# Cosine attention followed by a gated MLP: 73 narrow dummy matmuls become nine, seven of them 512 columns wide

## The chip, the cores and the metric

The kernel runs on one core of one Trainium2 chip. The metric is the device time of one launch in microseconds, as the median of several runs; lower is better. Three runs of the kernel before gave 273.07, 273.60 and 273.94 us, median 273.6.

## What is computed

Linear attention with cosine weights over 8 batches of 8 heads (576 positions, head size 64), then a two-layer MLP (512 to 2048 to 512) with a gate `h * sigmoid(beta * h)`:

```python
r = np.maximum(x, 0.0)                                   # phi(x), for q and k
phi = np.concatenate([r * cos_w, r * sin_w], axis=-1)
kv  = np.einsum('bhsf,bhsd->bhfd', k_p, v)
z   = np.sum(k_p, axis=2)
num = np.einsum('bhsf,bhfd->bhsd', q_p, kv)
den = np.einsum('bhsf,bhf->bhs', q_p, z)[..., None] + 1e-06
x   = (num / den).transpose(0, 2, 1, 3).reshape(4608, 512)
h   = x @ w_in
out = (h / (1 + np.exp(-beta * h))) @ w_out
```

## The kernel before

The 4608 tokens of the MLP are worked on in nine chunks of 512, each about one batch of attention long. TensorE (PE) does all products: k against v (`kv_mm`, L276), q against that result (`num_mm`, L297), both layers of the MLP (L386 and L621, and from the third chunk on a scheme with fewer products, L511 and L563) and many transposes. VectorE (DVE) and ScalarE (ACT) clip, scale, divide and move results out of PSUM; GpSimd (POOL) helps. All operations are issued in an order written by hand; each engine works through its own instructions in that order, and waits on semaphores where it needs another engine's result or a DMA.

The change concerns the first microseconds. While the first loads (`raw_q`, `raw_v`, `raw_k`, issued from the queue of SP in that order: q, first half of v, first half of k, second half of v, the rest of k, then weights) are on their way, this happens:

- DVE writes zeros into a tile of 512 columns that is later the tile S1 (the profile calls it S): 128 columns first (L145), two small constants (L147, L149), then the other 384 (L160). ACT makes cos and sin, DVE makes tan of the positions (L176).
- PE runs dummy matmuls on these zeros, by `warm_pe(count, w, bank)` at L673: `count` matmuls of a 128x128 weight of zeros on `w` columns of zeros (default 512), each overwriting `w` columns of one PSUM bank that nobody reads. L685 issues 58 of 48 columns, L700 six of 128, L701 nine of 48, and L704 one of 512.
- Between them stand real operations. L689: nine fp32 transposes that spread tan over the partitions; DVE copies the result to `tanr` (L694). L692: a transpose of beta. L235: nine transposes of the first half of q, after DVE clipped it to `qb` (L193), and nine of the second half after L704. ACT copies the turned q (L240), DVE multiplies it by `tanr` (L223).
- `warm_long` (L679) runs two more dummies, in fp32 on real columns of q; each shows as two matmuls in the trace.
- Then the first real products: L276 (kv of the first two heads of each group, waiting for k clipped by ACT, L192, and DVE, L193), ACT's copy (L286), L297, DVE's division (L308, L312, L319), the transposes of its result (L356), and the MLP's first layer (L386).

```python
zeros = S1.rearrange("q i t -> q (i t)")[:, 0:512]
nc.vector.memset(zeros[:, 0:P], 0.0)
...
nc.vector.memset(zeros[:, P:512], 0.0)
```

## Time and profile before

| | |
|---|---|
| median of 3 runs | 273.6 us (273.07 to 273.94) |
| span of the profiled execution (first to last instruction) | 272.7 us |
| PE busy, matmuls | 265.3 us, 97% |
| PEld busy (weight loads, overlapping PE) | 206.8 us, 76% |
| DVE busy | 224.0 us, 82% |
| ACT busy | 188.4 us, 69% |
| POOL busy | 68.3 us, 25% |

The span is of one profiled execution; its whole device time is not listed apart from the three runs. A line of the page or of the timeline names the line of the kernel (L675 is line 675), the engine, the operation, what is written from what, the sizes, and how often (x58). In the timeline the first two numbers are the start and the length in microseconds of a run of like instructions; the bracket at the end gives how long the engine was idle before it and who released it. A matmul's end is modelled: its record contains the drain of the array, so records of consecutive matmuls overlap, and the distance between two starts says what one costs. The chain of waits follows the execution back from its last instruction, at each step to what released it.

### The profile page before, as it was taken

To read this page: it belongs to the slowest core of one execution; us is meant where nothing else is said; L and a number is where in the kernel's file an instruction comes from. 1 tells how busy PE (TensorE), PEld (TensorE's weight loads), DVE (VectorE), ACT (ScalarE), POOL (GpSimd) and SP (SyncE) were. 2 spreads that over 40 slices of the span, in tenths; PEclk is the share of its full clock that TensorE was granted. 3 is DMA by queue.
4 is the path that set the end of the run, shared out by engine and by line. 5 is a ranking of instruction groups with operands and counts; after the bars stand their busy time and mean duration, and the time that the engine had idled before them with its cause. 6 is when DMAs were issued, how large, how long until landed. Compare 5 with 4: busy or idle time off the path is not lost.

```text
span 272.7 us, 8970 instructions
## 1 busy us (share of the span) xinstructions
PE 265.3 (97%) x3712; PEld 206.8 (76%) x3712; DVE 224.0 (82%) x596; ACT 188.4 (69%) x384; POOL 68.3 (25%) x89
## 2 busy tenths in 40 slices
PE   8899999999899999999999999999999999999994
PEld 8554455455784588888888888888888888888883
DVE  5989969499989889789989997899589768757852
ACT  4778777796419656899489966996696179428920
POOL 1444000510078000660085009300840060000001
PEclk9999999999999999999999999999999999999999
DMA  6999999999969999994589439943600570015005
GB/s 237 374 395 383 392 390 319 379 201 336 284 130 311 240 348 226 240 313 103 147 216 370 92 58 223 332 71 62 181 2 2 61 185 1 2 27 130 0 2 155
DMA packets 50681, 54.00 MB, mean 198 GB/s; under 512 B 31232, under 2 KB 31760, under 8 KB 50640
## 3 DMA queue, kind: packets, MB, share of 16 engines
q1 hardware_dynamic: 47504, 45.55, 59.1%
q0 software_dynamic: 2784, 7.61, 9.6%
q8 instruction: 29, 0.48, 0.7%
q10 hardware_dynamic: 352, 0.27, 0.4%
q14 instruction: 12, 0.10, 0.1%
HBM read 36.71 MB, written 9.44 MB: 169 GB/s over the span
## 4 chain that ended last, share of the span: by engine, by line
PE 85%; DVE 9%; DMA 3%; SPq 1%; issue 1%; ACT 1%; DVEq 0%
PE ps L621 32%; PE ps L511 27%; PE ps L386 10%; PE ps L544 5%; PE ps L563 4%; PE ps L297 3%; DMA raw_v<-in_v_dram 3%; PE ps L276 3%; DVE vb L219 1%; DVE xs L319 1%; DVE qs L223 1%; SPq L79 1%; DVE S L406 1%; DVE rk L193 1%; DVE qb L193 0%
## 5 line engine op out<-in xcount | busy, mean ns | idle before, releaser
L537 POOL DMA_DIRECT2D out_dram<-o_sb x58 | 33.9, 591 | 147.3 <-ACT o_sb L658 86.3
L420 ACT ACTIVATE g_t<-ps,beta 128x512 bf16<-128x512 f32 x96 | 60.3, 702 | 1.4 <-PE ps L511 1.3
L621 PEld LDWEIGHTS <-S 128*128 128x128 bf16 x448 | 43.4, 98 | 5.2
L511 PE MATMUL ps<-w_stage 128*128 128x256 bf16 x288 | 46.6, 272 | 0.1
L386 PE MATMUL ps<-xt,win 128*128 128x512 bf16 (+1 forms) x196 | 42.8, 375 | 0.1
L511 PEld LDWEIGHTS <-w_stage 128*128 128x128 bf16 x384 | 37.3, 98 | 5.1 <-issue 0.2
L487 DVE TENSOR_TENSOR ps<-ps,p 128x256 f32<-128x256 f32 x74 | 30.5, 428 | 8.6 <-PE ps L511 3.0
L394 ACT ACTIVATE g_t<-ps,beta 128x512 bf16<-128x512 f32 x48 | 32.3, 688 | 7.2 <-PE ps L386 7.1
L621 PEld LDWEIGHTS <-g_t 128*128 128x128 bf16 x336 | 32.3, 98 | 4.5 <-ACT g_t L420 0.4
L386 PEld LDWEIGHTS <-win 128*128 128x128 bf16 x196 | 18.7, 98 | 21.1 <-issue 0.5
L511 PE MATMUL ps<-xt,win 128*128 128x256 bf16 x192 | 32.9, 273 | 0.0
L511 PEld LDWEIGHTS <-win 128*128 128x128 bf16 x288 | 28.0, 98 | 3.4
L621 PE MATMUL ps<-wout,g_t 128*128 128x256 bf16 x224 | 28.9, 273 | 0.0
L406 DVE TENSOR_TENSOR S<-g_t 128x512 bf16<-128x512 bf16 (+1 forms) x66 | 25.7, 418 | 3.3 <-ACT g_t L420 1.7
L480 ACT COPY ps<-ps 128x256 f32<-128x256 f32 x62 | 22.6, 383 | 7.5 <-PE ps L621 4.0
L217 ACT ACTIVATE vb<-raw_v,sin 128x256 bf16<-128x256 f32 (+1 forms) x58 | 26.0, 503 | 1.5 <-DMA raw_v<-in_v_dram 1.5
L621 PE MATMUL ps<-T,S 128*128 128x256 bf16 x224 | 26.6, 273 | 0.0
L621 PE MATMUL ps<-wout,S 128*128 128x256 bf16 x224 | 26.4, 273 | 0.0
L319 DVE TENSOR_TENSOR xs<-ps,rden 128x768 bf16<-128x768 f32 (+4 forms) x26 | 22.8, 884 | 0.9 <-DVE rden L312 0.2
L223 POOL TENSOR_TENSOR qs<-qt,tanr 128x1152 bf16<-128x1152 bf16 x6 | 14.3, 2387 | 27.4 <-PE ps L563 21.0
L658 ACT COPY o_sb<-ps 128x512 f32<-128x512 f32 x11 | 6.3, 587 | 20.1 <-PE ps L621 20.1
L487 DVE TENSOR_TENSOR ps<-ps,u 128x256 f32<-128x256 f32 x36 | 15.3, 427 | 5.3 <-PE ps L511 3.3
(112 smaller groups left out, 414.7 us busy)
## 6 DMA issues: line engine op xcount, KB each, us to landing
raw_v<-in_v_dram SPq DMA_DIRECT2D x7, 1152.0 KB, 9.7
raw_k<-in_k_dram SPq DMA_DIRECT2D x7, 1152.0 KB, 9.5
raw_q<-in_q_dram SPq DMA_DIRECT2D x7, 1152.0 KB, 7.4
out_dram<-o_sb POOLq DMA_DIRECT2D x58, 128.0 KB, 4.5
w_stage<-in_moe_w_in_dram SPq DMA_DIRECT2D x3, 1024.0 KB, 12.8
w_stage<-in_moe_w_out_dram SPq DMA_DIRECT2D x2, 1024.0 KB, 7.9
w_stage<-in_moe_w_out_dram SPq DMA_DIRECT2D x4, 512.0 KB, 11.9
out_dram<-o_sb SPq DMA_DIRECT2D x10, 128.0 KB, 2.4
```

Source lines behind the costliest of these rows:

```text
L217: got = nc.scalar.activation(o, a, AF.Copy, scale=t[:, n : n + 1])
L223: return eng.tensor_tensor(dst.rearrange("q n (g p) -> q n g p", g=2), src.rearrange("q n (g p) -> q n g p", g=2), tanr[:, n0:n1].unsqueez ...
L319: nc.vector.tensor_tensor(o.rearrange("q j n s d -> q j (n s) d"), nv[:, :, a:z, :, 0:D].rearrange("q j n s d -> q j (n s) d"), rden[:, :, ...
L386: nc.tensor.matmul(ps[:, h_bank(c, jt), i * 64 : (i + w) * 64], lhsT=win[jt // 4][:, mi, (jt % 4) * P : (jt % 4 + 1) * P], rhs=xt[:, i : i ...
L394: return nc.scalar.activation(gs[c, jt // 4][:, jt % 4], ps[:, h_bank(c, jt)], AF.Silu, scale=beta[:, jt : jt + 1])
L406: return nc.vector.tensor_tensor(o, l, r, op=op)
L420: return nc.scalar.activation(gs[c, jt // 4][:, jt % 4], bank, AF.Silu, scale=beta[:, jt : jt + 1])
L480: return nc.scalar.copy(at("a", 0), at("b", 0))
L487: nc.vector.tensor_tensor(dst, at("b", 0), st["p5"], op=ALU.add)
L511: nc.tensor.matmul(dst, lhsT=l[:, g], rhs=r[:, :, g * HP : (g + 1) * HP], start=start and g == 0, stop=g == 1, skip_group_check=True)
L537: (eng or own).dma_start(out=out_v[bb, n][:, m0:m1], in_=o_sb[hf * HP : (hf + 1) * HP, m0:m1])
L621: nc.tensor.matmul(dst, lhsT=l(i), rhs=r[:, i], start=start and i == 0, stop=i == order[-1], skip_group_check=True)
```

## The change

Two places in the first microseconds. The 58 dummies of 48 columns ahead of the tan transposes become five of 512 columns. The six of 128 and nine of 48 columns ahead of the first q transposes become two of 512 and two of 48. Banks and positions in PE's order stay; the dummy at L704 and `warm_long` stay.

```diff
-    warm_pe(58, 48)
+    warm_pe(5)
...
     q_relu(0, 1)
-    warm_pe(6, 128, bank=2)
-    warm_pe(9, 48, bank=2)
+    warm_pe(2, bank=2)
+    warm_pe(2, 48, bank=2)
     q_turn_pe(0, 0, 4)
```

In columns, the first group goes from 58 x 48 = 2784 to 5 x 512 = 2560, the second from 6 x 128 + 9 x 48 = 1200 to 2 x 512 + 2 x 48 = 1120. PE has 64 matmuls and 64 weight loads less. The first wide dummy reads all 512 zero columns, and so waits for the memset at L160; the first narrow one read 48 and waited for an earlier one.

## The prediction

> **What bounds the kernel now.** I read the page first, then the windows, then the chain of waits, then the timeline of each engine up to 20 us.

> ```profile
> span 272.7 us, 8970 instructions
> PE 265.3 (97%) x3712; PEld 206.8 (76%) x3712; DVE 224.0 (82%) x596; ACT 188.4 (69%) x384; POOL 68.3 (25%) x89
> PEclk9999999999999999999999999999999999999999
> q8 instruction: 29, 0.48, 0.7%
> ```

> ```profile
> 19.00:69.00 50.00, 49.99 (x687) 26.21 (x684) 42.59 (x92) 39.00 (x66) 7.65 (x12) 1.00 1.05 346
> 71.00:269.00 198.00, 197.91 (x2690) 167.88 (x2688) 164.19 (x461) 135.67 (x290) 52.94 (x60) 1.00 0.59 147
> ```

> The windows (the columns are length, then PE, PEld, DVE, ACT and POOL busy, granted clock, DMA share, GB/s) show PE busy for 49.99 of 50 us and for 197.91 of 198. So from 19 us on the kernel is a solid block of TensorE work; the change touches nothing in it. What the change can move is the moment at which that block begins. The chain says what sets that moment:

> ```profile
> 3.16 9.06 DMA raw_v<-in_v_dram
> 12.22 0.02 issue
> 12.25 0.92 DVE vb L209
> ...
> 17.54 1.06 DVE xs L319 x2
> ...
> 18.65 0.40 PE ps L356 x4
> 19.04 3.03 PE ps L386 x18
> ```

> Up to 12.22 us it is a load, the second half of v (raw_v); from there to 18.6 us a run of VectorE work; PE takes over only at 18.65. The dummies, all before 7 us, are not in the chain.

> **The change on the timeline.** The PE rows of that stretch (start, length, what):

> ```profile
> 0.99 2.50 PE L675 MATMUL ps<-S 128*128 128x48 bf16 x58 [0.99 <-DVE zero_b L149]
> 3.56 1.19 PE L689 MATMUL ps<-identf,tan 64*128 64x64 f32 x9
> 4.68 0.29 PE L692 MATMUL ps<-identf,beta 16*128 16x16 f32 x1
> 4.90 1.18 PE L675 MATMUL ps<-S 128*128 128x128 bf16 x15
> 5.94 1.14 PE L235 MATMUL ps<-ident,qb 128*128 128x128 bf16 x9
> 6.88 0.63 PE L675 MATMUL ps<-S 128*128 128x512 bf16 x1
> 7.30 1.17 PE L235 MATMUL ps<-ident,qb 128*128 128x128 bf16 x9
> 8.26 2.30 PE L679 MATMUL ps<-raw_q,S 128*128 128x512 f32 x4
> 11.25 0.70 PE L276 MATMUL ps<-vb,rk 64*64 64x130 bf16 x36 [0.69 <-ACT rk L192]
> ...
> 16.81 1.46 PE L386 MATMUL ps<-xt,win 128*128 128x512 bf16 x6
> ...
> 22.26 7.94 PE L386 MATMUL ps<-xt,win 128*128 128x512 bf16 x36
> ```

> ```profile
> L675 PE MATMUL ps<-S x74: 214/215/634, 1.0 to 6.9; 128*128 128x48 bf16 x67, 128*128 128x128 bf16 x6, 128*128 128x512 bf16 x1
> L679 PE MATMUL ps<-raw_q,S x6: 592/592/1017, 8.3 to 13.6; 128*128 128x512 f32 x6
> ```

> *Prices.* A record's length contains its drain, so I price by the distance between starts. Narrow: (2.50 - 0.215) / 57 = 0.040 us. Wide: the one wide bf16 dummy starts at 6.88 and the next transpose at 7.30, so 0.42 us. The same 512 columns cost 7.94 / 36 = 0.22 us at 22 us. So before about 8.3 us PE runs at half its later rate, though the granted clock row shows full speed everywhere; the row evidently has nothing for this stretch, and I trust the spacing. The fp32 dummies of L679 date the turn: the longest, 1017 ns, is the first, and 592 the usual, so the rate doubled while they ran, between 8.3 and about 9.1 us.

> *First group, line 685.* Removed: 58 x 0.040 = 2.32 us. Added: 5 x 0.42 = 2.10 us. One wait is added. A narrow dummy reads 48 zero columns, which the first memset writes; a wide one reads all 512, so the first now waits for the second memset. DVE:

> ```profile
> 0.89 0.06 DVE L149 MEMSET zero_b<- 128x1 f32 x1
> 0.94 0.22 DVE L160 MEMSET S<- 128x192 uint32 x1
> ...
> 3.25 0.17 DVE L176 TENSOR_TENSOR tan<-eps,sin 128x9 f32<-128x9 f32 x1
> ...
> 4.36 0.85 DVE L694 COPY tanr<-ps 128x320 f32<-128x320 f32 x2 [0.37 <-PE ps L689]
> 5.13 0.75 DVE L193 TENSOR_SCALAR qb<-raw_q 128x1152 bf16<-128x1152 f32 x1
> ...
> 12.25 1.35 DVE L209 TENSOR_TENSOR vb<-raw_v,ps 128x1152 bf16<-128x1152 f32 x1 [0.19 <-DMA raw_v<-in_v_dram]
> ```

> That memset ends at 0.94 + 0.22 = 1.16; PE started 0.04 us after the one it waited for (0.89 + 0.06 to 0.99), so now about 1.20 in place of 0.99. Behind the waiting dummy stand only dummies and the L689 transposes. The wide group is through at 1.20 + 2.10 = 3.30. The transposes read tan, ready at 3.25 + 0.17 = 3.42, and began at 3.56; they keep 3.56 with 0.2 us to spare. On the path: 0. If a wide one cost its whole record (0.63) at the end, it would end at 1.20 + 4 x 0.42 + 0.63 = 3.51, still before 3.56. At the full rate (0.22) it ends at 2.3, and PE just idles. What would a miss cost? The tanr copy at 4.36 waits for these transposes, and DVE then has 0.19 us of idle before its 12.25 entry, where it waits for the load anyway; a delay d costs d - 0.19.

> *Second group, lines 700 and 701.* Removed: 6 of 128 and 9 of 48 columns, from 4.90 to 5.94, 1.04 us. Added: 2 x 0.42 + 2 x 0.040 = 0.92, so done at 5.82. The q transposes behind it read qb, which DVE has at 5.13 + 0.75 = 5.88, and started 0.06 after that. They stay at 5.94. Path: 0; the earliest they could gain is under 0.06, and the load at 12.22 hides it.

> *What is issued.* 64 matmuls and their 64 weight loads fall away, 128 PE instructions. The orders of POOL and SP are unchanged and those of DVE and ACT keep each instruction in its place. No DMA is moved past another.

> *The turn of the rate.* No row shows what makes it turn, so I bound it. Total dummy time before 6 us falls from 2.32 + 1.04 to 2.10 + 0.92 us, a tenth, in the same places; PE streams in both from 4.9 us to the L679 dummies with no pause above 0.1 us. I take an unchanged turn: 0. Earlier: the transposes of L235 would end earlier, but DVE, ACT and POOL all wait at 12.2 us for raw_v, so 0 as well. Later: the first rival.

> [...]

> *Sum.* 0 (first group) + 0 (second) + 0 (instructions) + 0 (rate) on the span of 272.7 us. The profiled execution's span lies 0.9 us below the median of the runs, 273.6, which I take as what lies around it plus run-to-run spread (0.87 us from 273.07 to 273.94). Forecast: 273.6 us, no change that can be told.

> **Rivals.**

> *A. The rate turns later; slower.* For it: the dummies begin 0.21 us later, are a tenth shorter, and the turn at 8.3 to 9.1 us came late already. Against it: the 18 transposes and the L679 dummies on real data, which precede the turn, are untouched. Place: L679 and L276. Three of the four L679 matmuls would take 1.017 in place of 0.592, +1.28 us, of which PE's idle 0.69 us before 11.25 takes part: with the drain of 0.16 off, they end at 8.26 + 2.30 + 1.28 - 0.16 = 11.68. L276 starts 0.43 late and, at half rate, its nine steps of (0.70 - 0.217) / 9 = 0.054 double, +0.48 (0.217 is the median L276 record). So its result is 0.91 late. ACT takes it:

> ```profile
> L276 PE MATMUL ps<-vb,rk x576: 214/217/242, 11.3 to 194.4; 64*64 64x130 bf16 x192
> 12.01 0.38 ACT L286 CAST kv<-ps 128x260 bf16<-128x260 f32 x1 [0.81 <-PE ps L276]
> 12.28 1.28 ACT L217 ACTIVATE vb<-raw_v,sin 128x128 bf16<-128x128 f32 x4
> 13.46 0.97 ACT L192 ACTIVATE rk<-raw_k 128x576 bf16<-128x576 f32 x2
> ```

> ACT then works without a pause to 13.46 + 0.97 = 14.43, so its rk comes at 15.34. The second L276 group started at 14.62, about 0.06 after DVE's rk; it would start at 15.4, 0.8 later, and the VectorE run behind it has some 0.1 of slack: +0.7 us, 274.3. If the rate turned only after the second L276 group and the eight transposes at 15.25, another 0.48 + 8 x 0.05 = 0.9: +1.6, 275.2. It decides from a turn later than about 10.7 us (below that the idle 0.69 us hides it), and passes 0.3% only when the second group is cold as well. Middle: 274.8. Chance 0.20.

> [...]

> *B. Instruction packets arrive at another moment; slower.* 7424 PE and PEld instructions over 29 packets of queue q8 are 256 each, so q8 feeds PE. Without 128 instructions every packet falls due half a packet later in the work. The first two of before came in these windows, 9 to 11 us and 18 to 19.5 us, when the loads filled the DMA engines:

> ```profile
> q8 instruction: 1, 0.02, 3.1%
> ...
> q8 instruction: 1, 0.02, 4.6%
> ```

> By the PE rows (two instructions each matmul), some 640 had run by 17.5 us with one packet landed, so at least 384, likely 512, were there at the start. In the changed program the 512th instruction is the old 640th, among the six matmuls from 16.81; its packet is asked for around the old 384th, near 13 us, not before 10. If it were as late as the old second packet, landing at 19.5, PE would stand from 17.5: 2.0 us, less some 0.3 that PE has until 18.65 for this work: +1.7, 275.3. Against it: PE shows no such wait in before. It decides where the packet takes over 4 us. Chance 0.12.

> *C. Faster.* For more than 0.3% the block would have to begin 0.8 us earlier, that is, raw_v land earlier or the VectorE run shorten; I see no row for it. It remains that the runs of before spread over 0.87 us and the changed kernel may land at their low end or beyond, 272.7 or so, if the rate turns earlier in each run. Chance 0.12.

> **How the numbers follow.** Forecast 0.56; A 0.20, B 0.12, C 0.12. 0.3% (0.8 us) is about what a measurement of this kernel tells from no change. Same 0.56, slower 0.20 + 0.12 = 0.32, faster 0.12. The range: its low end 272.8 leaves out most of C, its high end 275.0 the far ends of A and B, together no more than 0.2. The likeliest case alone is 273.1 to 274.3 (the lowest run, and A's small price).

> **What would show it.** Right: the first dummy at 1.2 us, five starts 0.42 apart, L689 still at 3.56, L235 at 5.94, DVE at 12.25 waiting for raw_v, PE's turns at 18.65. Wrong in the first group: L689 after 3.6. Wrong in the rate: wide dummies 0.22 apart, or L679 with more than one record at 1017. For A: L276 at 11.6 or later with steps of 0.11. For B: PE idle between 16.8 and 19.5 with no releaser, and q8 packets at other times. If the block begins at 18.65 as before and the time still moves, the cause lies where I did not look.

## The result, and the profile after

The changed kernel takes 280.11 us (median of 5, 279.56 to 280.79), the kernel before 273.76 us (5 runs). The ratio is 1.022, with a 95% interval of 1.021 to 1.024: 6.3 us slower.

The page of the changed kernel:

```profile
span 278.5 us, 8842 instructions
PE 266.7 (96%) x3648; PEld 205.2 (74%) x3648; DVE 224.2 (81%) x596; ACT 188.3 (68%) x384; POOL 68.4 (25%) x89
PEclk9977999999999999999999999999999999999998
```

The span grew by 5.8 us while PE's busy time grew by 1.4; the rest is waiting. The granted clock, full in all slices before, dips in the third and fourth slice (14 to 28 us). PE's timeline, with the same lines as before:

```profile
1.21 2.29 PE L675 MATMUL ps<-S 128*128 128x512 bf16 x5 [1.21 <-DVE S L160]
3.56 1.19 PE L689 MATMUL ps<-identf,tan 64*128 64x64 f32 x9
...
4.90 1.11 PE L675 MATMUL ps<-S 128*128 128x512 bf16 x4
5.94 1.14 PE L235 MATMUL ps<-ident,qb 128*128 128x128 bf16 x9
...
14.80 0.83 PE L356 MATMUL ps<-ident,xs 128*128 128x128 bf16 x8
15.56 0.23 PE L297 MATMUL ps<-kv,qt 64*64 64x65 bf16 x4
...
18.44 0.26 PE L297 MATMUL ps<-kv,qt 64*64 64x65 bf16 x2 [2.40 <-issue]
...
19.03 2.74 PE L386 MATMUL ps<-xt,win 128*128 128x512 bf16 x6
21.56 1.06 PE L356 MATMUL ps<-ident,xs 128*128 128x128 bf16 x8
22.41 4.15 PE L386 MATMUL ps<-xt,win 128*128 128x512 bf16 x18
26.75 9.67 PE L386 MATMUL ps<-xt,win 128*128 128x512 bf16 x44
...
107.75 0.49 PE L621 MATMUL ps<-T,S 128*128 128x256 bf16 x3 [1.09 <-issue]
```

The dummies do what was expected of them: the first at 1.21, L689 still at 3.56, L235 still at 5.94. The loss comes much later. In the middle of the second group of L297, PE stands for 2.40 us, released by "issue": no semaphore, nothing that the profile shows. After it PE is slower for a while. The rows of before for the same work are these:

```profile
16.01 0.22 PE L297 MATMUL ps<-kv,qt 64*64 64x65 bf16 x4
...
18.18 0.86 PE L356 MATMUL ps<-ident,xs 128*128 128x128 bf16 x8
18.88 3.19 PE L386 MATMUL ps<-xt,win 128*128 128x512 bf16 x18
```

The six of L386 take 2.74 us in place of 1.46, 1.9 times as long (the granted clock is 0.50 there), the eight of L356 1.06 in place of 0.86, and the next 18 of L386 4.15 in place of 3.19, as the granted clock comes back to 1.00 in the midst of them, at 24.35. A second such wait, 1.09 us, ends at 107.75.

The windows of the changed kernel cut at these moments (length, then busy time and count of PE, PEld, DVE, ACT and POOL, the granted clock, DMA share, GB/s):

```profile
0.00:16.04 16.04, 12.93 (x222) 7.51 (x222) 12.55 (x33) 10.72 (x23) 5.80 (x14) 1.00 0.89 322
16.04:18.44 2.40, 0.00 (x0) 0.00 (x1) 0.34 (x1) 0.77 (x2) 1.97 (x4) 0.81 1.03 386
18.44:24.35 5.91, 5.91 (x52) 3.32 (x53) 5.12 (x13) 1.59 (x4) 1.63 (x2) 0.50 1.05 385
16.04:17.50 1.46, 0.00 (x0) 0.00 (x0) 0.34 (x1) 0.77 (x2) 1.34 (x3) 1.00 1.02 380
```

During the wait the clock falls to half (mean 0.81, still 1.00 up to 17.50) and stays at 0.50 until 24.35. The price adds up by the distance between starts. From this group of L297 to L386's long run before takes 22.26 - 16.01 = 6.25 us, the changed kernel 26.75 - 15.56 = 11.19. The difference of 4.94 is 2.40 of wait and 2.54 of slower steps. PE had been 0.45 us ahead (15.56 against 16.01), as DVE began its work on the second half of v at 11.79 in place of 12.25, with no wait for that load; so the long run begins 4.49 us late. With the second wait, 1.09, that makes 5.58 of the 5.8 us of span; 0.2 stays unassigned.

Which resource stood still? Queue q8, which by its counts brings PE's instructions: it has 29 packets for before's 7424 matmuls and weight loads, 256 each, and 28 for the changed kernel's 7296. Two lines of the list of DMA queues; the first is before's in the window 9.9 to 10 us, the second the changed kernel's in 15.8 to 16 us. In the changed kernel there is no earlier one:

```profile
q8 instruction: 1, 0.02, 62.1%
...
q8 instruction: 1, 0.02, 31.7%
```

So the first packet starts 6 us later than before, and just ahead of the wait.

### The profile page after: what moved, and what is told of

It is laid out like the page before. It is cut to its first block, busy times and chain, and to the rows that moved or that the text cites. A ratio compares the mean times of both kernels' runs of the same rounds, so it can differ in the third digit from the quotient of the medians.

```text
span 278.5 us, 8842 instructions
## 1 busy us (share of the span) xinstructions
PE 266.7 (96%) x3648; PEld 205.2 (74%) x3648; DVE 224.2 (81%) x596; ACT 188.3 (68%) x384; POOL 68.4 (25%) x89
## 3 DMA queue, kind: packets, MB, share of 16 engines
q0 software_dynamic: 2784, 7.61, 9.5%
## 4 chain that ended last, share of the span: by engine, by line
PE 89%; DMA 5%; issue 2%; ACT 1%; SPq 1%; DVE 0%; ACTq 0%
PE ps L621 31%; PE ps L511 26%; PE ps L386 14%; PE ps L544 5%; PE ps L297 4%; PE ps L563 4%; PE ps L276 3%; DMA raw_q<-in_q_dram 3%; DMA raw_k<-in_k_dram 3%; PE ps L356 1%; SPq L79 1%; ACT qb L192 0%; PE ps L679 0%; PE ps L235 0%; ACT rk L192 0%
## 5 line engine op out<-in xcount | busy, mean ns | idle before, releaser
L386 PE MATMUL ps<-xt,win 128*128 128x512 bf16 (+1 forms) x196 | 45.0, 389 | 0.0
L386 PEld LDWEIGHTS <-win 128*128 128x128 bf16 x196 | 19.4, 101 | 22.2 <-issue 1.7
L511 PEld LDWEIGHTS <-win 128*128 128x128 bf16 x288 | 28.0, 98 | 3.4
L217 ACT ACTIVATE vb<-raw_v,sin 128x256 bf16<-128x256 f32 (+1 forms) x58 | 26.0, 505 | 0.8 <-DMA raw_v<-in_v_dram 0.8
L319 DVE TENSOR_TENSOR xs<-ps,rden 128x768 bf16<-128x768 f32 (+4 forms) x26 | 22.8, 884 | 0.9 <-DVE rden L312 0.2
L223 POOL TENSOR_TENSOR qs<-qt,tanr 128x1152 bf16<-128x1152 bf16 x6 | 14.3, 2386 | 28.6 <-DMA qt<-qb 22.1
L219 DVE TENSOR_SCALAR vb<-raw_v,cos 128x256 bf16<-128x256 f32 x63 | 20.1, 369 | 0.0
```

Of the source, the lines that this page charges most:

```text
L217: got = nc.scalar.activation(o, a, AF.Copy, scale=t[:, n : n + 1])
L219: got = nc.vector.tensor_scalar(o, a, scalar1=t[:, n : n + 1], scalar2=None, op0=ALU.mult)
L319: nc.vector.tensor_tensor(o.rearrange("q j n s d -> q j (n s) d"), nv[:, :, a:z, :, 0:D].rearrange("q j n s d -> q j (n s) d"), rden[:, :, ...
L386: nc.tensor.matmul(ps[:, h_bank(c, jt), i * 64 : (i + w) * 64], lhsT=win[jt // 4][:, mi, (jt % 4) * P : (jt % 4 + 1) * P], rhs=xt[:, i : i ...
L511: nc.tensor.matmul(dst, lhsT=l[:, g], rhs=r[:, :, g * HP : (g + 1) * HP], start=start and g == 0, stop=g == 1, skip_group_check=True)
```

## The experiments

Theory S (supply): PE runs dry of instructions, because with 128 instructions less ahead of the first products the next packet is asked for too late. Theory W: the wide dummies themselves do harm, through the rate of PE. Every kernel computes the reference in full; they differ in their dummies alone, g2 in the place of some weight loads alone. The dummy at L704, 512 columns wide, stays in all and is not counted. Times are medians in us; "before" is the kernel before in runs on the same chip beside them.

| run | dummies (columns) | time | ratio to before (95%) | issue waits of PE over 0.3 us |
|---|---|---|---|---|
| e1_pad64_early | 9, and 64 (8) behind L679 | 276.88 | 1.011 (1.006 to 1.016) | 1.86, 0.71 |
| e2_nine_narrow | 9, none wide | 278.60 | 1.017 (1.011 to 1.022) | 2.36, 1.04, 0.98 |
| e3_pad32_early | 9, and 32 (8) behind L679 | 282.79, one run | | 1.48, 2.94, 0.86, 0.42 |
| e4_pad64_late | 9, and 64 (8) at 30.7 us | 278.00, one run | | 2.42 |
| f1_73_of_8 | 73, all 8 | 273.59 | 1.000 (0.999 to 1.002) | none |
| f2_wide_66 | 66, four of 512 | 278.48 | 1.016 (1.011 to 1.021) | 2.24, 1.25, 1.30 |
| f4a_minus8 | 65, narrow | 278.38, one run | | 2.53, 0.75, 0.49, 1.56 |
| f4b_minus16 | 57, narrow | 280.41, one run | | 2.27, 3.11 |
| g1_120_of_8 | 120, all 8 | 278.85, one run | | 2.51 |
| g2_quiet_dma | 9 as changed, weights late | 282.93, one run | | none at 14 to 18 us; later 1.65, 1.04 |
| g3_wide_77 | 77, three of 512 | 273.81 | 1.001 (0.999 to 1.002) | none |
| g4_81_of_8 | 81, all 8 | 275.10 | 1.004 (1.003 to 1.006) | 0.93 |

Before had a median of 273.84 beside the e runs, 273.76 beside the f runs and 273.53 beside the g runs.

**First four: number or width?** The edits, here and below, are shortened to their calls.

```diff
 e1:  warm_long(2)  +  warm_pe(64, 8)          (on the changed kernel)
 e2:  warm_pe(5, 48) ... warm_pe(2, 128, bank=2); warm_pe(2, 48, bank=2)
 e3:  warm_long(2)  +  warm_pe(32, 8)          (on the changed kernel)
 e4:  if slot == 10: warm_pe(64, 8)            (on the changed kernel)
```

> The kernel before with only nine dummies and none of them wide: 5 of 48 columns, then 2 of 128 and 2 of 48. PE has as many instructions as in the changed kernel. Theory S: the first packet falls at 15 to 16 us, PE stands near 16 us for 1.5 to 2.5 us, time 279 to 281. Theory W: no wide dummies, no wait at 16 us, time 273.5 to 274.5. If the dummies matter by their activity alone (rate turns later than 9 us, no wait in the products), 274 to 275.5.

> The changed kernel with its nine dummies kept, and 64 more of 8 columns behind warm_long, in PE's idle time ahead of L276 (9.6 to 11.1 us). Theory S (supply: with 128 instructions less, the first q8 packet is asked for in the middle of the products of 12 to 16 us, and PE stands without instructions from 16.04 to 18.44): the packet starts near 10 us again, no issue wait at 16 us, no half rate from 17.5 to 24.4, time 273.6 to 274.7 (the 64 take at most 64 x 0.040 = 2.6 us, of which 1.4 are idle time). Theory W (the wide dummies themselves, by turning the rate at 7.3 us in place of 9.0 and letting it fall back at 17.5): the half rate and the wait stay, time 280 to 281.

> The changed kernel with 32 dummies of 8 columns behind warm_long, half of what was removed. Theory S: the boundary of the packets lies 64 instructions earlier in the work than in the changed kernel, so the first packet is asked for near the start of L297 at 12.2 us or before; the wait at 16 us is gone or under 1 us, and the half rate with it; 273.6 to 277. Theory W: 280 as with no padding.

> The changed kernel with 64 dummies of 8 columns late, in the first layer of the MLP at slot 10, near 28 us. PE has as many instructions in all as before. Theory S: what counts is the number ahead of the products at 12 to 16 us, so the wait at 16 us and the half rate stay, and the second issue wait of the changed kernel (106.66, 1.09 us) goes, since all packets behind 28 us are where they were before: 280 + 64 x 0.03 - 1.1 = 280 to 282. Were it the program's length in all, the wait at 16 us would go: 274 to 276.

e2 decides against W: none of its nine dummies is wide, and the same wait stands at the same place. (Its 278.60 us lies just under the expected 279.) Its timeline row, and its window up to the wait:

```profile
18.14 0.22 PE L297 MATMUL ps<-kv,qt 64*64 64x65 bf16 x2 [2.36 <-issue]
```

```profile
0.00:15.79 15.79, 11.28 (x222) 7.66 (x222) 12.30 (x33) 10.61 (x23) 5.81 (x14) 1.00 0.89 317
```

222 matmuls and 222 weight loads stand ahead of the wait, exactly as in the changed kernel. e4 agrees with S on both counts: the wait at 16 us stays and the one near 107 us is gone. Its 278.00 us is below the expected 280 to 282; the half rate was there, but only from about 19.6 to 23.0 us (its first six of L386 take 1.90 us, against 2.74 in the changed kernel and 1.46 in before).

e1 and e3 missed. e1 was to be cured and lost 1.1%. Its rows:

```profile
16.34 0.53 PE L276 MATMUL ps<-vb,rk 64*64 64x130 bf16 x22 [1.86 <-issue]
```

```profile
0.00:14.47 14.47, 12.03 (x222) 7.37 (x222) 10.93 (x30) 9.32 (x20) 4.69 (x13) 1.00 0.88 315
```

The padding moved the wait from L297 to L276, other code, but it again falls behind 222 + 222. So the place of the wait is a count of instructions, 444 of these two kinds, whatever they are. What the padding did not mend is the moment of the request: e1's packet starts between 13.7 and 14.0 us, because the 64 were issued at 9.4 to 11 us, where before's first packet had already started at 9.9. The number of instructions matters, and the time by which PE has taken them. e3 was the slowest of these four: it waits 1.48 us behind the 444, and its halved padding puts a later boundary at 71.87 us, where PE stands 2.94 us:

```profile
74.81 1.46 PE L563 MATMUL ps<-T,S 128*128 128x256 bf16 x6 [2.94 <-issue]
```

**Next four: activity, and where the edge is.** With 444 as the halt and 256 instructions a packet, my estimate is that PE asks for the next packet about 256 instructions earlier; no row shows the request itself. (The expectations that follow count five other instructions of PE along: their 448th or 449th is the end of these 444.)

```diff
 f1:  warm_pe(58, 8) ... warm_pe(15, 8, bank=2)
 f2:  warm_pe(40, 8); warm_pe(3) ... warm_pe(1, bank=2); warm_pe(22, 8, bank=2)
 f4a: warm_pe(50, 48)    in place of warm_pe(58, 48), on the kernel before
 f4b: warm_pe(42, 48)    in place of warm_pe(58, 48), on the kernel before
```

> The kernel before with the same 73 dummies, all of them 8 columns wide (584 columns in place of 3984). Theory S, sharpened by the first four runs: PE holds two packets of 256 instructions; it asks for the next when it has begun the 192nd one that the trace shows, and stands at the 448th unless that packet is there, which takes about 6 us while the loads run. So only the number of PE instructions ahead of the first products counts: the 192nd is begun near 7.4 us as before, no issue wait at 14 to 18 us, 273.3 to 275. If columns (activity) counted: the rate turns later than 11 us and the time is 275 or more.

> Four wide dummies and 62 of 8 columns: first group 40 of 8 columns, then 3 of 512; second group 1 of 512, then 22 of 8. Theory S: 66 dummies in the early places are 14 instructions less than before, the 192nd is then an early one of warm_long's or the last q transposes (7.5 to 9 us), no wait at 14 to 18 us, 273.3 to 275. Theory W (wide dummies do the harm): 277 or more.

> The kernel before with 50 in place of 58 narrow dummies in the first group, 16 instructions less. Theory S: the 192nd instruction is the old 208th, still ahead of L276 (old 216th), begun by 8.3 us; no wait, 273.3 to 275. A cost in proportion to the removed dummies (64 cost 6.3 us) would give 0.8 us more: 274.5.

> The same with 42 of 58, 32 instructions less. Theory S: the 192nd is the old 224th, an L276 that waits for k until 11.25 us; the packet is asked for 3 us later than with 50, starts near 14.7, and PE stands at its 448th (in the second L276 group, 15 us) until about 17.3: an issue wait of 1.5 to 2.5 us, 276 to 280. In proportion: 275.3.

f1 keeps the count and cuts the columns from 3984 to 584: same time as before, to 0.2%. So what the dummies compute, and how long they keep PE busy, is worth nothing that can be measured here. Their number is. f1's timeline row, and its queue q8 in the window 9.8 to 10 us, where before has its first packet too:

```profile
0.99 1.71 PE L675 MATMUL ps<-S 128*128 128x8 bf16 x58 [0.99 <-DVE zero_b L149]
```

```profile
q8 instruction: 1, 0.02, 30.8%
```

f4a was expected to be fast and was not; the edge is nearer than I thought. Its wait, its window up to the wait, and its first q8 packet, which is in 14.3 to 14.6 us:

```profile
16.92 0.41 PE L276 MATMUL ps<-vb,rk 64*64 64x130 bf16 x14 [2.53 <-issue]
```

```profile
0.00:14.40 14.40, 12.16 (x222) 9.09 (x222) 10.99 (x31) 9.45 (x20) 4.44 (x12) 1.00 0.88 314
14.40:16.92 2.52, 0.00 (x0) 0.00 (x0) 1.69 (x4) 0.02 (x1) 2.23 (x4) 1.00 1.05 401
```

```profile
q8 instruction: 1, 0.02, 19.4%
```

Eight dummies less, 16 instructions, and the first packet comes 4.5 us later. Ahead of L276, before has 212 matmuls and weight loads (58 + 9 + 1 + 15 + 9 + 1 + 9 + 4 matmuls, each with a load), f4a 196. L276 waits for k until 11 us, and PE takes nothing beyond it. So the request most likely falls between the 198th and the 212th: before gets past that point ahead of the wait for k, f4a, f4b (180) and f2 (198) only after it. Before then stands at most 14 instructions from the edge. f2, with wide and f4b, with narrow dummies, wait alike at L276 (2.24 and 2.27 us), and f2's expectation failed for the same reason as f4a's. f4b waited there as expected, but a second wait of 3.11 us took it to 280.41, just over its 280.

The windows also give an estimate of what a refill takes, with this edge as the moment of the request. In the changed kernel 210 of these instructions have begun by 12.46 us:

```profile
0.00:12.46 12.46, 9.39 (x103) 5.38 (x107) 9.11 (x24) 7.41 (x14) 3.80 (x12) 1.00 0.85 302
```

PE runs again at 18.44, 6.0 us later. f4a has begun 215 by 10.93 us and runs again at 16.92, also 6.0 us later. The 234 instructions up to the halt last the changed kernel only until 16.04, and the rest is the wait. In before, with the request over by 10 us at the latest (its packet starts at 9.9), the 444th instruction is begun only at 14.76.

**Last four: too many, a quiet DMA, and a cure.**

```diff
 g1:  warm_pe(82, 8) ... warm_pe(38, 8, bank=2)
 g3:  warm_pe(44, 8); warm_pe(3) ... warm_pe(30, 8, bank=2)
 g4:  warm_pe(62, 8) ... warm_pe(19, 8, bank=2)
 g2:  (on the changed kernel, shortened; `behind` makes the DMA wait for the copy)
-    load_w("in", 0, 2)                        (behind the first loads of k)
-    for i in range(1, 4): load_w("in", i)     (ahead of the first num_mm)
+    held = kv_take((1,), 6, eng="act")
+    load_w("in", 0, 2, behind=held)
+    for i in range(1, 4): load_w("in", i)
```

> The kernel before with 120 dummies of 8 columns in place of 73 (82 in the first group, 38 in the second), 94 PE instructions more. Theory S: more is as bad as less. The first packet is asked for early and lands in time, but the second is then asked for near the old 370th instruction, in the first L297 group at 12.7 us, about 2 us before its place in before (14.7); it starts near 16.2, and PE stands at the 705th (the old 611th, in the second L297 group) from about 16.4 to 18.8: an issue wait of 1.5 to 2.5 us there, 276 to 281. If only too few instructions did harm: 273.3 to 275.

> The changed kernel (nine dummies) with the weight loads of the first layer held back until ACT has taken the second kv result, near 15 us. Theory S with the full DMA engines as the cause of the slow packet: from 12 us the engines have nothing to do, the packet asked for at 11 to 12.5 us starts within 1 us of that, not at 15.8, and PE has no issue wait at 14 to 18 us. The first layer starts some 4 us late for want of weights, so the time is 276 to 281 and says little. If a packet takes 6 us in any case, the wait at 16 us stays.

> Three wide dummies behind 44 of 8 columns in the first group, 30 of 8 columns in the second: 77 dummies, 8 PE instructions more than before, with 1888 columns in place of 3984. Theory S: no issue wait at 14 to 18 us, 273.3 to 274.5, ratio to before 0.997 to 1.003. Theory W: 277 or more.

> 81 dummies of 8 columns (62, then 19), 16 PE instructions more than before. Theory S: the first packet is asked for a little earlier and with more margin, the second near the old 448th in the second L276 group as before, so no wait; 273.2 to 274.5. If before now and then misses its packet, as single runs of 275 may say, the highest of these runs is lower than that, and the median 0 to 0.3 us below before.

g1 stands where it should, in L297, behind 350 + 350 = 700 instructions, and 444 + 256 is 700:

```profile
19.09 0.21 PE L297 MATMUL ps<-kv,qt 64*64 64x65 bf16 x1 [2.51 <-issue]
```

```profile
0.00:16.58 16.58, 14.11 (x350) 10.38 (x350) 12.42 (x33) 10.74 (x23) 5.92 (x15) 1.00 0.91 322
```

So 120 dummies do the same harm, one packet on. g2 shows why a packet takes so long. Its windows, and q8 in its window 13 to 13.4 us:

```profile
12.00:13.00 1.00, 0.77 (x65) 0.72 (x65) 1.00 (x1) 1.00 (x5) 0.49 (x1) 1.00 0.01 2
13.00:14.00 1.00, 1.00 (x4) 0.19 (x4) 0.92 (x7) 1.00 (x4) 0.00 (x0) 1.00 0.05 16
14.00:15.00 1.00, 1.00 (x40) 0.85 (x40) 1.00 (x3) 0.78 (x4) 0.00 (x0) 1.00 0.00 0
15.00:16.00 1.00, 0.96 (x67) 0.72 (x67) 0.12 (x1) 1.00 (x3) 0.00 (x0) 1.00 0.00 0
```

```profile
q8 instruction: 1, 0.02, 13.7%
```

The dummies are the nine of the changed kernel, but from 12 us the DMA engines are idle (share 0.00 to 0.05, where the changed kernel has 0.93 to 1.11). The packet starts some 2.6 us earlier than in the changed kernel, PE takes 67 matmuls from 15 to 16 us, where the changed kernel has 42, and the wait behind the 444 is gone. Its total of 282.93 us, over the expected 281, is longer because the weights come late: PE stands 4.36 us for them, until 20.58. The later waits of 1.65 and 1.04 us stay; the DMA engines are idle only in this early stretch.

g3 is the cure with wide dummies kept: 77 in all, with 2128 columns (the 1888 of the expectation are the first group's alone), no issue wait, 273.81 us and a ratio of 1.001, where the changed kernel has 1.022. g4, meant as before with more margin, missed: it gets past 16 us, but 16 more instructions move a later boundary into the MLP's first chunk, and PE stands there:

```profile
44.84 0.59 PE L544 MATMUL ps<-wout,g_t 128*128 128x512 bf16 x2 [0.93 <-issue]
```

This wait is 0.93 of the 1.57 us that g4 loses; what makes up the rest stays open. No version beat the kernel before; two equal it (f1, g3).

## Why the prediction was wrong

The forecast of 273.6 us fell short of 280.11. Step by step:

- *What bounds the kernel.* Right in part. The forecast held that the change touches nothing in the block from 19 us on; but the second wait (1.09 us, to 107.75) lies inside it, and the half rate reaches into it until 24.35. And the chain, which names VectorE up to 18.65, hides how little time PE had to spare there. Before's window shows PE busy for 3.84 of 4.03 us, so a wait of PE in this stretch is paid almost in full:

```profile
14.62:18.65 4.03, 3.84 (x117) 2.37 (x117) 3.80 (x10) 2.67 (x9) 3.32 (x5) 1.00 1.07 398
```

- *First and second group.* Right to the hundredth: first dummy at 1.21 (1.20 predicted), L689 at 3.56, L235 at 5.94. Path 0, as said.
- *Rate.* Right that its turn at the start costs nothing: it turned earlier (the second L235 group, at 7.29 us, takes 0.67 us in place of 1.17), and f1, with a seventh of the columns, is as fast as before. Rival A did not happen. (Its step of 0.05 us for the eight L356 transposes fits no row of theirs: from 15.25 to 16.01 they are about 0.09 apart. Nothing hangs on it.) That the rate would fall back in a wait (granted 0.50 from soon after 17.50 to 24.35) was in no term.
- *Instructions: "0 (instructions)".* This is the term that failed. I saw that 128 PE instructions fall away and wrote nothing for it in the sum. They cost 2.40 + 1.09 us of waiting, and behind the first wait another 2.54 of slower steps.
- *Rival B* named the mechanism: packets of 256, the 128 instructions that move them, the full DMA engines, a wait of 2.0 us from 17.5, and its sign (PE idle with no releaser). Measured: 2.40 us, from 16.04. Its chance of 0.12 was too low and its price of 1.7 too small. Against it I held that "PE shows no such wait in before". That was no evidence: before escapes by some 14 instructions at most, as f2 and f4a show. B's count was off as well. By it the old second packet was asked for at the old 512th instruction, taken at 16.02 us, and landed by 19.5, within 3.5 us, under the 4 from which B decides. The halts put the request earlier, and 6.0 us pass from there until PE runs again.
- B also left out the fall of the clock behind a wait, and the other boundaries later in the work (106.66 us), which the same 128 instructions move.

The later halts agree with packets of 256: 444 and 700 (g1) are 256 apart, 1206 (f4a, counted in the window up to its wait that ends at 47.27) and 1974 (f4b, up to its wait of 3.11 from 72.64) lie six below such steps, and from the edge of the request to the halt PE has 232 to 246 instructions left, about one packet. That PE holds two packets, as the expectation of f1 has it, was an estimate: the changed kernel's PE ran 444 instructions before its first packet, started at 15.8 us at the earliest, was of use, and 444 is more than one packet of 256 and less than two. No run shows the request, or what PE holds, directly. In the changed kernel the refill was not hidden: PE stood for 2.40 us.

What is shown: the place of the waits is a count of instructions (e1, e2, f4a and f4b halt behind the same 444), width and activity play no part (e2, f1, g3), and the load on the DMA engines is what makes the first packet late (g2, one run). What is argued only: that the 2.54 us of slower steps are due to the half rate alone; no run had the wait of the changed kernel at full clock from 18 to 24 us with all else the same. f4a comes near: a wait of 2.53 us and the clock at 1.00 through it. e2's four runs speak for it: one kernel, 277.55 us at a mean granted clock of 1.000, 278.49 at 0.999, 278.71 at 0.991 and 280.39 at 0.986. Not shown is what makes the later waits: no run had quiet DMA engines there.

## What to carry to other kernels

Count the instructions of an engine that issues very many, not only their time: here 128 instructions less, of dummies that are not in before's chain of waits, moved the start of the first packet from 9.9 to 15.8 us, with the DMA engines full (share 0.93 to 1.11) and a burst of short matmuls running, and PE stood for 2.40 us. The sign in this case was an idle stretch of PE released by "issue" in the middle of a group of like instructions, with a packet of q8 just ahead; compare how many instructions went before it in several variants. Where such a kernel is tuned, check the neighbours, since a good time can be a matter of where the boundaries happen to fall: here eight dummies less cost 4.6 us (f4a, one run) and eight more 1.57 us (g4).

## What the runs showed of the hardware that was not expected

- The moment at which PE's rate doubles was not set by the dummies alone. With the same nine dummies the changed kernel ran its first L235 group, at 5.94 us, in 1.14 us, e1 at 5.93 in 0.68, about what the second group takes at the later rate (0.67); these are L235's records in e1 (minimum, median and longest in ns):

```profile
L235 PE MATMUL ps<-ident,qb x36: 219/219/230, 5.9 to 42.3; 128*128 128x128 bf16 x36
```

```profile
18.14:19.25 1.11, 1.11 (x34) 0.71 (x35) 0.60 (x5) 0.00 (x0) 0.00 (x0) 1.00 1.05 387
19.30:22.65 3.35, 3.35 (x17) 1.92 (x15) 3.25 (x8) 1.59 (x4) 0.64 (x1) 0.50 1.06 389
```

What sets that moment is not shown.

- PE resumed about 2.5 us after the packet started (15.8 to 16 us, then 18.44; in f4a 14.3 to 14.6, then 16.92), while the DMA engines were full (share 1.03 and 1.05 in the two waits).
